# Other DRAM layouts for the block inverse, and separate tiles for values and receptance

## The chip, the cores and the metric

One core of one Trainium2 chip runs the kernel. TensorE multiplies matrices, VectorE, ScalarE and GpSimd work element by element, and SyncE (SP in the profile) issues most transfers between the core's SBUF and DRAM. The time is device microseconds of one execution. The kernel before took 1365.18 us, the median of three runs from 1364.78 to 1365.78.

## What is computed

Three layers follow one another, all in float32: a recurrence over 768 steps for 4 batches of 8 heads with a 40 x 40 state each, and two MLPs on its output, 3072 tokens of width 320 with 2048 hidden units.

```
for t in range(S):
    y[:, :, t] = einsum('bhd,bhde->bhe', rt, state)
    Sa = einsum('bhde,bhe->bhd', state, at)
    state = state * wt[:, :, None, :] - einsum('bhd,bhe->bhde', Sa, bt)
    state = state + einsum('bhd,bhe->bhde', vt, kt)
x = y.transpose(0, 2, 1, 3).reshape(B * S, H * D)
x = relu(x @ w_in) ** 2 @ w_out                      # first MLP
h = x @ w2_in
out = (h * clip(h + 3, 0, 6) / 6) @ w2_out           # second MLP
```

The weights come as 64-bit words and are converted to pairs of float32 in the kernel.

## The kernel before

The 768 steps are cut into 12 chunks of 64. A chunk of one batch is a *block* i = 4c + b (48 of them); it holds 8 heads as NP = 4 pairs p of two halves h, a half being 64 of the 128 partitions. Inside a block the recurrence is a unit lower triangular system of 64 steps for each head, and its inverse is needed before the block's states can be formed. The inverse is made for a whole chunk at once: 16 units u = (b, p), two halves h and two diagonal 32 x 32 blocks f of each 64 x 64 triangle, 64 triangles in all.

Where things lie:

- `TB` (ring of three, one per chunk) holds the triangles of a chunk, partition = 64 h + 32 f + row, free = unit and column. `f1a` (L595 to L606) makes two of its blocks with TensorE, ScalarE copies them, and after every second block L605 stores both to DRAM, tile `DT`, ordered row, half, unit, column.
- `inv_gen` (L626) reads the diagonal blocks back, one triangle per partition, into `ML` (L635, four transfers: the two lane groups q, each with f = 0 and 1). A lane group q computes every second column of each inverse. 31 steps of two instructions each (L645 multiply, L648 subtract) run on VectorE; chunk 1 has tiles of its own (`inv_e`) and runs on GpSimd. L650 transposes the result, L652 and L653 store it to `DIT` and `DI`, and L658 and L660 read it back to `TB` and to `AI` with rows on partitions.
- `merge_p` and `merge_x` (L663, L673) join the two 32 x 32 inverses of a head with TensorE; merge_p (L669) is the first reader of `AI` and of the returned `TB`.
- `VR` (ring of three) holds a block's values and receptance, `[104, 2, NP, 128]`, the two halves of a head pair in opposite columns; `load_main` (L547) loads it with one transfer per half (L552), and `VS` with another (L551). `umm` writes the block's solution into the free half of the value part, `gmm` (L708) multiplies value part by receptance part, `ys` (L728, L731) forms outputs and the state that follows (L735 to L737).

What runs when is written out by hand. A *slot* is one block: the string `ORDER` names its steps, and each `M` in it is one piece of the first MLP (`fill`), after which five steps of the waiting inverse are put on VectorE (`tick`). Blocks enter `f1` eight ahead of `ys`. After the fourth block of a chunk is prepared its inverse is begun: L635 is put on SyncE's queue, and the first L645 comes three slots' ends later in VectorE's program. Every engine takes its instructions in the order of the program, so a VectorE instruction that waits holds all that stand behind it, and a SyncE transfer that waits holds all later transfers of that queue. Besides this traffic SyncE's queue holds the loads of weight words (L83), the stores of converted weights (L137), the stores of the recurrence's output (L743) and the loads of the MLP's input (L188, L191). GpSimd loads the next block's inputs (L545) and ScalarE the converted weights (L162).

From about 285 to 870 us recurrence and first MLP run together; after that the second MLP runs alone.

Of the kernel before, what the change touches and what calls it, by code (L numbers as in the profile page):

```python
# [8 lines left out]
FP32 = mybir.dt.float32  # L9
# [460 lines left out]
def rwkv_moe_moe2_kernel(ctx, tc, pre_in, vr_in, v_in, nat, ident_d, mask_d, cst_d, w1_in, w1_out, w2_in, w2_out, out,  # L470
# [34 lines left out]
    AI = ring([128, NB, NP, 32], 2, "AI")  # L505
    VR = ring([104, 2, NP, 128], 3, "VR")
    RHS = ring([128, NP, 40], 1, "RHS")
    GV = ring([128, NP, 2, 104], 1, "GV")
    VS = ring([128, NP, 2, 40], NB, "VS")
    STK = ring([104, NP, 40], NB, "STK")  # L510
# [12 lines left out]
    U = NB * NP  # L523
    DT = [dram.tile([64, 2, U, 64], FP32, name=f"DT{k}") for k in range(2)]
    DI = [dram.tile([2 * U, 32, 2, 16], FP32, name=f"DI{k}") for k in range(2)]
    DIT = [dram.tile([4 * U, 32, 32], FP32, name=f"DIT{k}") for k in range(2)]

# [19 lines left out]
    def load_main(i):  # L547
        c, b = divmod(i, NB)
        for h, P in enumerate((PA, PB) if i < NS else ()):
            PV = slice(64, 128) if h == 0 else slice(0, 64)  # L550
            nc.sync.dma_start(out=VS[i % NB][PV, :, h, :], in_=v_in[c, b, h])  # L551
            nc.sync.dma_start(out=VR[i % 3][P, :, :, 64 - 64 * h:128 - 64 * h], in_=vr_in[c, b, h])  # L552

# [41 lines left out]
    def f1a(i):  # L595
        ps = f1_ps[i] = bank([128, NP, 128])
        rk, kb, tb = RK[i % RL], kb_of(i), tb_of(i)
        for p in range(NP):
            nc.tensor.matmul(ps[:, p, :], kb[:, p, :], rk[0:104, p, :], start=True, stop=True)  # L599
        for h in range(2):  # L600
            p = 64 * h
            nc.scalar.copy(out=tb[p:p + 64], in_=ps[p:p + 64, :, p:p + 64])
        c, b = divmod(i, NB)
        if b % 2:
            nc.sync.dma_start(out=DT[c % 2].rearrange("s h u t -> h s (u t)")[:, :, (b - 1) * NP * 64:(b + 1) * NP * 64],  # L605
                              in_=TB[c % 3][:, b - 1:b + 1].rearrange("p s a t -> p (s a t)"))  # L606

# [18 lines left out]
    def inv_gen(c, eng=nc.vector, ml=ML, inv=INV, tm=TMP):  # L626
# [6 lines left out]
        for q in range(2):  # L633
            for f in range(2):
                nc.sync.dma_start(out=ml[64 * q + 2 * U * f:64 * q + 2 * U * f + 2 * U],  # L635
                                  in_=dt_[32 * f:32 * f + 32, :, :, 32 * f:32 * f + 32].rearrange("s h u t -> (h u) s t"))
        iv = inv.rearrange("p a b -> p (a b)")
# [13 lines left out]
        for q in range(2):  # L651
            nc.sync.dma_start(out=dit.rearrange("l (k q) t -> q l k t", q=2)[q], in_=ml[64 * q:64 * q + 64, 0:16])  # L652
            nc.sync.dma_start(out=di[:, :, q, :], in_=inv[64 * q:64 * q + 2 * U])  # L653
        yield 1
        for h in range(2):
            (nc.gpsimd if c else nc.vector).memset(tb[64 * h + 32:64 * h + 64, :, 0:32], 0.0)
        for h, f, P, l in blocks:
            nc.sync.dma_start(out=tb[P, :, 32 * f:32 * f + 32], in_=dit[l:l + U].rearrange("u s t -> s u t"))  # L658
            if f == 0:
                nc.sync.dma_start(out=ai[P], in_=di[l:l + U].rearrange("u s q k -> s u (q k)"))  # L660
        yield
# [21 lines left out]
    def rhs(i):  # L683
        ps = bank([128, NP, 40])
        rk, vs = RK[i % RL], VS[i % NB]
        for p in range(NP):
            for h in range(2):
                nc.tensor.matmul(ps[64 * h:64 * h + 64, p, :], rk[:, p, 64 * h:64 * h + 64], vs[:, p, h, :],
                                 start=True, stop=True)
        nc.scalar.copy(out=RHS[0], in_=ps)  # L690

    def umm(i):
        ps = bank([104, NP, 64])
        tb, o = tb_of(i), VR[i % 3][:, 0]
        for p in range(NP):
# [9 lines left out]
    def gmm(i):  # L705
        ps = bank([128, NP, 128])
        for p in range(NP):
            nc.tensor.matmul(ps[:, p, :], VR[i % 3][:, 0, p, :], VR[i % 3][:, 1, p, :], start=True, stop=True)  # L708
        nc.vector.tensor_tensor(out=gv_of(i)[:, :, :, 0:64], in0=ps.rearrange("p a (h t) -> p a h t", h=2)[:, :, ::-1],
# [3 lines left out]
    def vumm(i):  # L713
        ps = bank([128, NP, 2, 64])
        pf = ps.rearrange("s p h e -> s p (h e)")
        for p in range(NP):
            nc.tensor.transpose(pf[:, p, 0:104], VR[i % 3][:, 0, p, :], ident[0:104, 0:104])
        nc.scalar.copy(out=gv_of(i)[:, :, :, 64:104], in_=ps[:, :, :, 0:40])

    def ys(i):  # L720
        ps = bank([104, NP, 104])
        c, b = divmod(i, NB)
        ktt, gv, sb, r0 = KT[i % (lag + 1)], gv_of(i), SB[b], VR[i % 3][:, 1]

# [4 lines left out]
        for p in range(NP):  # L729
            for h, P in enumerate((PA, PB)):  # L730
                nc.tensor.matmul(ps[P, p, 0:64], sb[P, p, :], r0[P, p, 64 - 64 * h:128 - 64 * h], start=False,  # L731
                                 stop=(p == NP - 1))
# [12 lines left out]
    def st(i):  # L745
# [9 lines left out]
        for h, P in enumerate((PA, PB)):  # L755
            nc.scalar.copy(out=nxt[P, :, h, :], in_=STK[b][P])

# [95 lines left out]
    with tc.manual_schedule():  # L853
# [45 lines left out]
        for k in range(0, NB, 2):  # L899
            pre_two(k)  # L900
            f1a(k)
            f1a(k + 1)
        for x in (VS[0], VR[0]):
            nc.vector.memset(x, 0.0)
# [7 lines left out]
        for k in range(NB):  # L912
            f1b(k)
            kt(k)
        for x in VS[1:] + VR[1:] + STK + SB:
            nc.gpsimd.memset(x, 0.0)
# [159 lines left out]
```

## Time and profile before

| what | value |
|---|---|
| median of the runs | 1365.18 us |
| the profiled execution | 1360.24 us, its span 1358.5 us |
| busy: TensorE, its weight loads, VectorE | 86%, 73%, 63% of the span |
| busy: ScalarE, GpSimd | 45%, 30% |
| mean granted TensorE clock | 0.915 of full speed |
| DMA packets | 253021, of which 201687 under 512 bytes |
| bytes moved | 146.97 MB, 108 GB/s over the span |

A busy share says how much of the span an engine had work; a wait says which other engine or transfer ended the idle time before an instruction. A transfer's row stands on the queue that issued it, and its length there is the issue alone; the landing shows in the row of the instruction that waits for it, or as a DMA piece of the chain of work. [...]

### The profile page before, as it was taken

To read this page: it belongs to the slowest core of one execution; us is meant where nothing else is said; L and a number is where in the kernel's file an instruction comes from. 1 tells how busy PE (TensorE), PEld (TensorE's weight loads), DVE (VectorE), ACT (ScalarE), POOL (GpSimd) and SP (SyncE) were. 2 spreads that over 40 slices of the span, in tenths; PEclk is the share of its full clock that TensorE was granted. 3 is DMA by queue.
4 is the path that set the end of the run, shared out by engine and by line. 5 is a ranking of instruction groups with operands and counts; after the bars stand their busy time and mean duration, and the time that the engine had idled before them with its cause. 6 is when DMAs were issued, how large, how long until landed. Compare 5 with 4: busy or idle time off the path is not lost.

```text
span 1358.5 us, 25814 instructions
## 1 busy us (share of the span) xinstructions
PE 1162.4 (86%) x9682; PEld 991.6 (73%) x9682; DVE 852.1 (63%) x1857; ACT 609.6 (45%) x1456; POOL 409.0 (30%) x601
## 2 busy tenths in 40 slices
PE   3177677898989798989888999978879999999994
PEld 3167567786768676877777788856668999999994
DVE  7838897858485848494949383359975434344432
ACT  4245555453445344544544343346654434344331
POOL 5685545343434343534343200024530000000000
PEclk9657867898999898999998899988989999999998
DMA  4546657554655555736463544265541010101000
GB/s 125 115 99 190 166 139 165 158 130 118 129 140 135 119 128 138 152 106 137 140 145 90 114 135 112 76 204 183 160 128 30 22 37 15 51 8 44 3 18 23
DMA packets 253021, 146.97 MB, mean 108 GB/s; under 512 B 201687, under 2 KB 216663, under 8 KB 252887
## 3 DMA queue, kind: packets, MB, share of 16 engines
q1 hardware_dynamic: 234327, 91.63, 28.7%
q10 hardware_dynamic: 13824, 37.75, 9.0%
q0 software_dynamic: 4736, 15.84, 4.1%
q8 instruction: 79, 1.29, 0.4%
q14 instruction: 55, 0.45, 0.1%
HBM read 115.30 MB, written 29.88 MB: 107 GB/s over the span
## 4 chain that ended last, share of the span: by engine, by line
PE 49%; DVE 17%; DMA 17%; SPq 4%; issue 4%; ACT 4%; POOL 3%; DVEq 0%; ACTq 0%; POOLq 0%
PE h L221 9%; DMA DT<-TB 6%; PE h L223 4%; PE o L262 4%; PE o L261 4%; PE o L260 4%; DVE TMP L645 3%; DVE INV L648 3%; PE o L248 2%; PE a L599 2%; PE h L224 2%; PE h L225 2%; DMA xr<-X 2%; PE o L249 2%; PE o L250 2%
## 5 line engine op out<-in xcount | busy, mean ns | idle before, releaser
L239 DVE TENSOR_TENSOR gs<-g,gs 128x512 fp32r<-128x512 f32 x192 | 149.7, 780 | 77.9 <-ACT gs L233 65.9
L645 DVE TENSOR_TENSOR TMP<-ML,INV 128x126 f32<-128x126 f32 (+22 forms) x341 | 111.6, 327 | 80.9 <-DMA ML<-DT 72.6
L614 POOL TENSOR_TENSOR RK<-RK,mask 64x256 f32<-64x256 f32 x96 | 74.9, 780 | 235.7 <-ACT RK L613 210.4
L231 DVE SCALAR_TENSOR_TENSOR g<-r,h 128x512 f32<-128x512 f32 x96 | 66.0, 687 | 120.2 <-ACT r L230 120.1
L105 POOL TENSOR_TENSOR bits<-res,bits 128x384 int32<-128x384 int32 (+1 forms) x64 | 67.8, 1064 | 204.9 <-DMA wl<-LI 122.3
L260 PE MATMUL o<-w_out,gs 128*128 128x320 f32 x384 | 119.5, 311 | 7.5 <-ACT os L837 5.4
L236 DVE TENSOR_TENSOR g<-r 128x512 f32<-128x512 f32 x96 | 65.7, 684 | 88.3 <-ACT r L235 88.2
L262 PE MATMUL o<-w_out,gs 128*128 128x320 f32 x384 | 120.0, 312 | 0.7 <-DVE gs L239 0.7
L230 ACT ACTIVATE r<-h,cst 128x512 f32<-128x512 f32 x96 | 66.1, 688 | 121.1 <-PE h L225 115.6
L261 PE MATMUL o<-w_lout,gs 128*128 128x320 f32 x384 | 119.3, 311 | 0.0
L648 DVE TENSOR_TENSOR INV<-INV,TMP 128x126 f32<-128x126 f32 (+22 forms) x341 | 111.7, 328 | 9.4 <-DMA VR<-in_vr_dram 0.4
L233 ACT CAST gs<-g 128x512 fp32r<-128x512 f32 x96 | 59.6, 620 | 82.9 <-DVE g L231 82.9
L575 POOL TENSOR_TENSOR RK<-IN,EE 40x256 f32<-40x256 f32 x82 | 67.3, 821 | 89.8 <-DVE EE L563 86.2
L221 PE MATMUL h<-xm,wl 128*128 128x512 f32 x192 | 78.5, 409 | 17.7 <-DMA wl<-LI 17.7
L235 ACT ACTIVATE r<-h 128x512 f32<-128x512 f32 x96 | 57.1, 594 | 81.4 <-PE h L225 71.9
L248 PE MATMUL o<-gs,wo_hi 128*128 128x512 f32 x192 | 88.7, 462 | 1.1 <-DVE os L837 1.1
L700 ACT ACTIVATE VR<-a 40x256 f32<-40x256 f32 x96 | 36.3, 378 | 109.4 <-PE a L698 108.9
L221 PE MATMUL h<-xm,wi_hi 128*128 128x512 f32 x192 | 84.8, 442 | 0.6 <-ACT xm L207 0.6
L260 PEld LDWEIGHTS o<-w_out,gs 128*128 128x128 f32 x384 | 72.6, 189 | 13.0 <-ACT os L837 5.8
L250 PE MATMUL o<-gs,wl 128*128 128x512 f32 x192 | 80.9, 421 | 1.2 <-DMA wl<-LO 1.2
L590 POOL TENSOR_TENSOR KBt<-IN,RV 104x256 f32<-104x256 f32 x78 | 72.9, 954 | 29.6 <-DVE INV L648 10.4
L249 PE MATMUL o<-gs,wo_hi 128*128 128x512 f32 x192 | 80.8, 421 | 0.1
(160 smaller groups left out, 2942.6 us busy)
## 6 DMA issues: line engine op xcount, KB each, us to landing
wl<-LI ACTq DMA_DIRECT2D x48, 384.0 KB
wl<-LO ACTq DMA_DIRECT2D x48, 384.0 KB
IN<-in_pre_dram POOLq DMA_DIRECT2D x37, 418.0 KB, 5.4
bits<-in_moe_w_in_dram SPq DMA_DIRECT2D x32, 384.0 KB
bits<-in_moe_w_out_dram SPq DMA_DIRECT2D x32, 320.0 KB
VR<-in_vr_dram SPq DMA_DIRECT2D x96, 80.0 KB
DT<-TB SPq DMA_DIRECT2D x24, 256.0 KB
xr<-X SPq DMA_DIRECT2D x12, 512.0 KB
```

Source lines behind the costliest of these rows:

```text
L221: nc.tensor.matmul(h, w[p][:, k], xm[:, k], start=(k + p == 0), stop=False)
L239: nc.vector.tensor_tensor(out=gs[:, 1], in0=g, in1=gs[:, 0].bitcast(FP32), op=ALU.subtract)
L248: nc.tensor.matmul(acc[d], hi, gs[:, 0], start=a, stop=False)
L249: nc.tensor.matmul(acc[d], hi, gs[:, 1], start=False, stop=False)
L250: nc.tensor.matmul(acc[d], lo, gs[:, 0], start=False, stop=z)
L260: nc.tensor.matmul(acc[q], gs[:, 0, s], hi, start=a, stop=False)
L261: nc.tensor.matmul(acc[q], gs[:, 0, s], lo, start=False, stop=False)
L262: nc.tensor.matmul(acc[q], gs[:, 1, s], hi, start=False, stop=z)
L590: e.tensor_tensor(out=kb_of(i)[:, :, 64 * x:64 * x + 64], in0=kb[:, :, x, :], in1=rr, op=ALU.mult)
L614: nc.gpsimd.tensor_tensor(out=o, in0=o, in1=mask[P].unsqueeze(1).to_broadcast([64, NP, 64]), op=ALU.mult)
L645: eng.tensor_tensor(out=tmp, in0=ml[:, s, s + 1:32].unsqueeze(2).to_broadcast([128, n, w]), in1=inv[:, s, 0:w].unsqueeze(1).to_broadcast([ ...
L648: eng.tensor_tensor(out=inv[:, s + 1:32, 0:w], in0=inv[:, s + 1:32, 0:w], in1=tmp, op=ALU.subtract)
```

## The change

- `DT` is laid out as diagonal block f, half, unit, row, column and holds the diagonal blocks alone. L605's one transfer per two blocks becomes four (half by diagonal block), and the read for a lane group q is one transfer of 64 triangles of 4 KB.
- `DIT` and `DI` have the lane group q as outermost dimension, so that the two stores of each are contiguous per triangle. The return reads then take one lane group each: eight transfers to `TB` (every second partition) where four stood, four to `AI` where two stood.
- `VR` is split into `VU` (values and solution) and `RZ` (receptance, halves outermost), and `VS` has its halves outermost. Values, receptance and `VS` are loaded with three transfers per half instead of two.

```diff
-    VR = ring([104, 2, NP, 128], 3, "VR")
+    VU = ring([104, NP, 128], 3, "VU")
+    RZ = ring([104, 2, NP, 64], 3, "RZ")
...
-    VS = ring([128, NP, 2, 40], NB, "VS")
+    VS = ring([128, 2, NP, 40], NB, "VS")
...
-    DT = [dram.tile([64, 2, U, 64], FP32, name=f"DT{k}") for k in range(2)]
-    DI = [dram.tile([2 * U, 32, 2, 16], FP32, name=f"DI{k}") for k in range(2)]
-    DIT = [dram.tile([4 * U, 32, 32], FP32, name=f"DIT{k}") for k in range(2)]
+    DT = [dram.tile([2, 2, U, 32, 32], FP32, name=f"DT{k}") for k in range(2)]
+    DI = [dram.tile([2, 2 * U, 32, 16], FP32, name=f"DI{k}") for k in range(2)]
+    DIT = [dram.tile([2, 4 * U, 16, 32], FP32, name=f"DIT{k}") for k in range(2)]
...
-            nc.sync.dma_start(out=VS[i % NB][PV, :, h, :], in_=v_in[c, b, h])
-            nc.sync.dma_start(out=VR[i % 3][P, :, :, 64 - 64 * h:128 - 64 * h], in_=vr_in[c, b, h])
+            nc.sync.dma_start(out=VS[i % NB][PV, h], in_=v_in[c, b, h])
+            nc.sync.dma_start(out=VU[i % 3][P, :, 64 - 64 * h:128 - 64 * h], in_=vr_in[c, b, h, :, 0])
+            nc.sync.dma_start(out=RZ[i % 3][P, 1 - h], in_=vr_in[c, b, h, :, 1])
...
-            nc.sync.dma_start(out=DT[c % 2].rearrange("s h u t -> h s (u t)")[:, :, (b - 1) * NP * 64:(b + 1) * NP * 64],
-                              in_=TB[c % 3][:, b - 1:b + 1].rearrange("p s a t -> p (s a t)"))
+            tb = TB[c % 3].rearrange("p s a t -> p (s a) t")
+            un = slice((b - 1) * NP, (b + 1) * NP)
+            for h in range(2):
+                for f in range(2):
+                    nc.sync.dma_start(out=DT[c % 2][f, h, un].rearrange("u s t -> s u t"),
+                                      in_=tb[64 * h + 32 * f:64 * h + 32 * f + 32, un, 32 * f:32 * f + 32])
...
-            for f in range(2):
-                nc.sync.dma_start(out=ml[64 * q + 2 * U * f:64 * q + 2 * U * f + 2 * U],
-                                  in_=dt_[32 * f:32 * f + 32, :, :, 32 * f:32 * f + 32].rearrange("s h u t -> (h u) s t"))
+            nc.sync.dma_start(out=ml[64 * q:64 * q + 4 * U], in_=dt_.rearrange("f h u s t -> (f h u) s t"))
...
-            nc.sync.dma_start(out=dit.rearrange("l (k q) t -> q l k t", q=2)[q], in_=ml[64 * q:64 * q + 64, 0:16])
-            nc.sync.dma_start(out=di[:, :, q, :], in_=inv[64 * q:64 * q + 2 * U])
+            nc.sync.dma_start(out=dit[q], in_=ml[64 * q:64 * q + 64, 0:16])
+            nc.sync.dma_start(out=di[q], in_=inv[64 * q:64 * q + 2 * U])
...
-            nc.sync.dma_start(out=tb[P, :, 32 * f:32 * f + 32], in_=dit[l:l + U].rearrange("u s t -> s u t"))
-            if f == 0:
-                nc.sync.dma_start(out=ai[P], in_=di[l:l + U].rearrange("u s q k -> s u (q k)"))
+            for q in range(2):
+                nc.sync.dma_start(out=tb[P.start + q:P.stop:2, :, 32 * f:32 * f + 32],
+                                  in_=dit[q, l:l + U].rearrange("u k t -> k u t"))
+                if f == 0:
+                    nc.sync.dma_start(out=ai[P, :, 16 * q:16 * q + 16], in_=di[q, l:l + U].rearrange("u s k -> s u k"))
...
-            nc.tensor.matmul(ps[:, p, :], VR[i % 3][:, 0, p, :], VR[i % 3][:, 1, p, :], start=True, stop=True)
+            nc.tensor.matmul(ps[:, p, :], VU[i % 3][:, p, :], RZ[i % 3][:, :, p, :], start=True, stop=True)
```

The other readers of `VR` and `VS` take the new names and dimensions; the memsets at the start that cleared a `VR` clear its `VU` and its `RZ`.

The engines that compute keep their order. SyncE's queue is what moves. First the place where chunk 6's blocks are stored and read back. A row is an issue: destination, source, shape, and xN for N alike. Numbers behind a name tell the copies of a tile apart. Before:

```order
L551 DMA VS_139<-in_v_dram 64x4x40
L552 DMA VR_136<-in_vr_dram 40x8x64
L551 DMA VS_139<-in_v_dram 64x4x40
L552 DMA VR_136<-in_vr_dram 40x8x64
L605 DMA DT_164<-TB_129 2x64x512
L635 DMA ML<-DT_164 32x32x32 x4
```

And now, on the same queue at the same place:

```order
L552 DMA VS_142<-in_v_dram 64x160
L553 DMA VU_136<-in_vr_dram 40x4x64
L554 DMA RZ_139<-in_vr_dram 40x256
L552 DMA VS_142<-in_v_dram 64x160
L553 DMA VU_136<-in_vr_dram 40x4x64
L554 DMA RZ_139<-in_vr_dram 40x256
L612 DMA DT_167<-TB_129 32x8x32 x4
L641 DMA ML<-DT_167 64x1024 x2
```

Six loads stand where four did, the store is four transfers instead of one, the read two instead of four; the order among them is the same.

The second place stands just ahead of the first: the return of the inverse of chunk 5, behind the output store of the slot. Before, on SyncE's queue:

```order
L743 DMA X_2_59<-XT_148 40x4x128 x2
L658 DMA TB_131<-DIT_169 32x16x32
L660 DMA AI_133<-DI_167 32x16x32
L658 DMA TB_131<-DIT_169 32x16x32
L660 DMA AI_133<-DI_167 32x16x32
L658 DMA TB_131<-DIT_169 32x16x32 x2
```

And now:

```order
L750 DMA X_2_59<-XT_151 40x4x128 x2
L664 DMA TB_131<-DIT_172 16x16x32
L667 DMA AI_133<-DI_170 32x16x16
L664 DMA TB_131<-DIT_172 16x16x32
L667 DMA AI_133<-DI_170 32x16x16
L664 DMA TB_131<-DIT_172 16x16x32
L667 DMA AI_133<-DI_170 32x16x16
L664 DMA TB_131<-DIT_172 16x16x32
L667 DMA AI_133<-DI_170 32x16x16
L664 DMA TB_131<-DIT_172 16x16x32 x4
```

Twelve issues stand where six did; the last piece of `AI` is the eighth of them, where it was the fourth.

## Rows read from the trace of the kernel before

**Rows 1.** Busy time by stretch: us, engines' busy us (instructions), clock, DMA share, GB/s.
```profile
285.00:870.00 585.00, 535.78 (x5520) 440.43 (x5520) 370.13 (x945) 269.30 (x717) 190.64 (x292) 0.95 0.52 126
...
292.00:322.00 30.00, 24.11 (x258) 19.63 (x258) 14.05 (x40) 10.29 (x28) 9.85 (x16) 0.89 0.57 134
...
763.00:803.00 40.00, 38.23 (x381) 31.12 (x381) 23.42 (x66) 18.94 (x48) 3.20 (x7) 0.96 0.47 121
sum 280.00, PE 245.60 PEld 201.66 DVE 162.14 ACT 125.64 POOL 95.42; mean PE 30.70 PEld 25.21 DVE 20.27 ACT 15.71 POOL 11.93
```

**Rows 2.** Waits, 285 to 870 us: engine, line <- releaser: total us, times, longest.
```profile
DVE TMP L645 <- DMA ML<-DT: 71.4, 8, 11.9
...
PE a L751 <- DVE STK L736: 27.2, 10, 5.9
```

**Rows 3.** Timeline, 411 to 446 us: start, length, engine, line, operation [idle before <-releaser].
```profile
418.19 0.31 SPq L658 DMA_DIRECT2D TB<-DIT  x1
...
420.35 4.87 SPq L658 DMA_DIRECT2D TB<-DIT  x2
...
426.35 0.65 PE L669 MATMUL a<-AI,TB 32*64 32x32 f32 x16
...
428.45 0.57 SPq L605 DMA_DIRECT2D DT<-TB  x1
...
439.79 1.06 PE L708 MATMUL a<-VR 104*128 104x128 f32 x8
439.84 2.27 SPq L635 DMA_DIRECT2D ML<-DT  x4
...
440.78 0.65 PE L669 MATMUL a<-AI,TB 32*64 32x32 f32 x16
...
445.58 0.19 DVE L645 TENSOR_TENSOR TMP<-ML,INV 128x31 f32<-128x31 f32 x1 [11.84 <-DMA ML<-DT]
```

**Rows 4.** Busy time by stretch of 3 us, right after that wait.
```profile
443.00:446.00 3.00, 0.00 (x0) 0.00 (x0) 0.33 (x2) 0.00 (x0) 0.00 (x0) 0.66 0.81 100
446.00:449.00 3.00, 1.73 (x7) 1.52 (x8) 2.83 (x13) 0.80 (x3) 0.22 (x1) 0.50 0.27 71
```

**Rows 5.** Transfers on the chain that ended last: start, us, what.
```profile
41.20 9.94 DMA DT<-TB
...
381.23 4.40 DMA xr<-X
...
495.73 9.41 DMA DT<-TB
...
814.67 4.38 DMA DI<-INV
...
963.32 2.34 DMA bits<-in_moe_w_out_dram
...
994.89 4.12 DMA X<-os
```

**Rows 6.** Issues on SyncE by line: ns min/median/max, first and last start.
```profile
L551 SPq DMA_DIRECT2D VS<-in_v_dram x96: 552/585/2672, 34.5 to 846.1; - x96
...
L552 SPq DMA_DIRECT2D VR<-in_vr_dram x96: 777/800/2431, 35.5 to 846.8; - x96
...
L658 SPq DMA_DIRECT2D TB<-DIT x48: 307/487/3173, 65.2 to 821.0; - x48
```

**Rows 7.** Timeline of the start, GpSimd's inverse and what stands behind it.
```profile
57.05 0.24 POOL L645 TENSOR_TENSOR inv_e<-inv_e 128x31 f32<-128x31 f32 x1 [9.65 <-DMA inv_e<-DT]
...
88.92 1.02 DVE L109 SCALAR_TENSOR_TENSOR res<-bits 128x384 f32<-128x384 f32 x1 [7.58 <-POOL bits L105]
...
92.33 1.62 PE L728 MATMUL a<-GV,KT 128*64 128x104 f32 x16 [7.00 <-DVE GV L709]
```

**Rows 8.** Waits of VectorE, 110 to 160 us.
```profile
DVE res L97 <- DMA bits<-in_moe_w_out_dram: 4.9, 1, 4.9
```

**Rows 9.** The page's DMA queues: packets, MB, share of 16 engines.
```profile
q1 hardware_dynamic: 234327, 91.63, 28.7%
```

More of the change, by code (lines that the diff above doesn't have):

```diff
@@ L687, in rhs @@
             for h in range(2):
-                nc.tensor.matmul(ps[64 * h:64 * h + 64, p, :], rk[:, p, 64 * h:64 * h + 64], vs[:, p, h, :],
+                nc.tensor.matmul(ps[64 * h:64 * h + 64, p, :], rk[:, p, 64 * h:64 * h + 64], vs[:, h, p, :],
                                  start=True, stop=True)
@@ L693, in umm @@
         ps = bank([104, NP, 64])
-        tb, o = tb_of(i), VR[i % 3][:, 0]
+        tb, o = tb_of(i), VU[i % 3]
         for p in range(NP):
@@ L716, in vumm @@
         for p in range(NP):
-            nc.tensor.transpose(pf[:, p, 0:104], VR[i % 3][:, 0, p, :], ident[0:104, 0:104])
+            nc.tensor.transpose(pf[:, p, 0:104], VU[i % 3][:, p, :], ident[0:104, 0:104])
         nc.scalar.copy(out=gv_of(i)[:, :, :, 64:104], in_=ps[:, :, :, 0:40])
@@ L722, in ys @@
         c, b = divmod(i, NB)
-        ktt, gv, sb, r0 = KT[i % (lag + 1)], gv_of(i), SB[b], VR[i % 3][:, 1]
+        ktt, gv, sb, r0 = KT[i % (lag + 1)], gv_of(i), SB[b], RZ[i % 3]
         PQ = (slice(0, 64), PB)
@@ L730, in ys @@
             for h, P in enumerate((PA, PB)):
-                nc.tensor.matmul(ps[P, p, 0:64], sb[P, p, :], r0[P, p, 64 - 64 * h:128 - 64 * h], start=False,
+                nc.tensor.matmul(ps[P, p, 0:64], sb[P, p, :], r0[P, 1 - h, p], start=False,
                                  stop=(p == NP - 1))
@@ L755, in st @@
         for h, P in enumerate((PA, PB)):
-            nc.scalar.copy(out=nxt[P, :, h, :], in_=STK[b][P])
+            nc.scalar.copy(out=nxt[P, h], in_=STK[b][P])
     gens = deque()
@@ L902, in rwkv_moe_moe2_kernel @@
             f1a(k + 1)
-        for x in (VS[0], VR[0]):
+        for x in (VS[0], VU[0], RZ[0]):
             nc.vector.memset(x, 0.0)
@@ L914, in rwkv_moe_moe2_kernel @@
             kt(k)
-        for x in VS[1:] + VR[1:] + STK + SB:
+        for x in VS[1:] + VU[1:] + RZ[1:] + STK + SB:
             nc.gpsimd.memset(x, 0.0)
```

## The prediction

> **What bounds the kernel now.** I read the page first (TensorE is the busiest engine by far), then the busy time by stage, then the waits of that stage, and last the timeline around one wait. The stage from 285 to 870 us, where recurrence and first MLP run together, has TensorE busy 535.78 of 585 us at a granted clock of 0.95 [rows 1]. So a gain has to come from its 49 us of idle time or from its clock. Its waits name two places: VectorE sits 71.4 us, in 8 pieces, before L645 until ML<-DT has landed, and TensorE sits 27.2 us before L751 for VectorE [rows 2]. They are one event, once for each chunk's inverse. SyncE stores the blocks (L605, DT<-TB), waits for the store, issues four reads of them (L635, ML<-DT), and VectorE, which takes its work in order, stands at the first step of the inverse.
>
> One event in full [rows 3]: the store is issued at 428.45, the first read only at 439.84, and VectorE starts at 445.58 after 11.84 us of waiting, so since 433.74. TensorE goes on with work that doesn't need VectorE until 441.43 (its last matmul group before the gap is the one at 440.78); 7.7 us of such a wait are covered, the rest is idle time of TensorE. [...]
>
> What all eight cost: the eight stretches of 30 or 40 us that begin with the store hold 280 us, TensorE busy 245.60 of them, so 34.4 idle [rows 1]. The other 305 us of the stage have 535.78 - 245.60 = 290.2 busy, 14.8 idle, 4.9%; at that rate the stretches would idle 13.6, so the excess is 20.8 us. The clock of the eight stretches, weighted by length, is 0.931 (rows from 0.89 to 0.98; the first and the last of the eight stand in [rows 1]); with 0.95 for the whole stage the other 305 us have 0.967. The difference over 280 us is 10 us of full-speed work. Together about **31 us** hang on this wait.
>
> **The change part by part.** VectorE, ScalarE, GpSimd and TensorE keep the order of their instructions; VR gives way to VU and RZ, and three memsets of it become six of half the size at the start, those of GpSimd ahead of its wait of 9.65 us for chunk 1's blocks [rows 7]. What changes is SyncE's queue, 633 rows before and 777 after with repeats joined, and the shape of its transfers.
>
> *The store of blocks.* One transfer of 256 KB becomes four of 32 KB that carry the diagonal blocks alone, in pieces of 128 bytes instead of 2 KB. Before, it takes 9.41 to 11.39 us from issue to the read that waits for it [rows 3, 5]. That is not what 256 KB cost in general: X<-os, 256 KB from 128 partitions, took 4.12 [rows 5]. The store's outermost dimension is the half, 2 long; after, it is 32 lanes. [...] New cost: three issues of 0.57 ahead of the last [rows 3], then the landing of small pieces, between 2.34 (a load of weight words, the fastest landing I quote) and 4.38 (DI<-INV, stores of 64-byte pieces) [rows 5]: 4.0 to 6.1 us. It saves 3.3 to 7.4; I take 5.2, the middle, since the store resembles DI<-INV in pieces but each of the four carries half the bytes.
>
> *The reads.* Four of 128 KB in 128-byte pieces become two of 256 KB in 4 KB pieces. Before: 445.58 - 439.84 = 5.74 us from first issue to VectorE's start [rows 3]. After: one issue of 0.3 to 0.6 and a landing between 2.34 (384 KB) and 4.40 (xr<-X, 768 KB in three) [rows 5], 2.7 to 5.0. It saves 0.7 to 3.0; I take 2.
>
> *What SyncE does ahead of the store.* The loads of values and receptance go from four to six per block. Before 2 x (0.585 + 0.800) = 2.77 us of issue [rows 6]. The values become one run per lane, the receptance too, and the third keeps strided halves with one dimension less. I take 0.4, 0.4 and 0.585 (a run of few dimensions costs between the 0.31 minimum of L658 and 0.585): 2.77, no change; bounds -0.4 to +1.9. The return of the inverse (TB<-DIT, AI<-DI) goes from six issues to twelve, of 0.487 each [rows 6]: 2.9 us more, in the slot just before the store. In the event above the burst began at 418.19 and the two last issues alone took 4.87, so the queue was held by the transfers and not by issuing [rows 3]; part of the 2.9 is then covered. I take 2 later; bounds 0 and 4.
>
> Sum for one event: 5.2 + 2 - 2 = **5.2 us earlier**, bounds -1 and 10. The mean wait of 71.4 / 8 = 8.9 us becomes 3.7, and the longest, 11.9, becomes 6.7. Both are inside the 7.7 us that TensorE covers, so nearly all of the 31 us come back: I take **28**; next late in these stretches is TensorE's own work. Bounds: 2 if an event moves by under 1 us, 43 if the 14.8 us idle in the rest of the stage, which follow from VectorE catching up after its wait, mostly go as well.
>
> *The start.* Chunk 1's inverse runs on GpSimd. Its store takes 9.94 us from 41.20 [rows 5], GpSimd waits 9.65 and starts at 57.05; behind its 62 steps stands the bits addition that VectorE's L109 waits 7.58 us for, and behind that the mask L709 for which TensorE waits 7.00 [rows 7]. Two stores become eight and the read moves as above, so the steps begin 5 to 8 us earlier and the 7.00 shrink by as much: **6**, bounds 0 and 7. The first inverse gains nothing: VectorE had other work until about when its blocks came.
>
> *Weight conversion, 110 to 285 us.* Loads of weight words are queued on SyncE behind the same store and reads; VectorE waited 4.9 us once for such words [rows 8], and for the stores of rests as well. I take **4**, bounds 0 and 10.
>
> *What it adds.* The merge of a block needs the first four reads of the inverse before and the first eight now, about 4 x 0.487 = 2 us later. In the event above the merge came at 426.35, 8.2 us after the burst began [rows 3]; eight issues (3.9) and a landing of up to 4.4 just fit. At the first and last inverse there is no such room: **-2**, bounds 0 and -40 (next part). The receptance operand of L708 is read in two runs of 64; no row shows that apart; the eight instructions of a block take 1.06 us [rows 3], and I take no change, at most a tenth of it, 5 us over 48 blocks. Packets of SyncE's queue, 234,327 for 28.7% of the engines' span [rows 9], fall by roughly 90,000 (4096 to 128 per inverse for ML alone), which is a gain that I don't count.
>
> Sum: 28 + 6 + 4 - 2 = **36 us**. The profiled execution took 1360.24 us, 1358.5 of it span; less 36 that is 1324. The median of the runs is 4.9 above it, 1365.18, and so **1329**.
>
> **Rivals.** *Small pieces eat the gain.* The change is meant to make pieces larger, but the block store goes from 2 KB to 128 bytes, and AI from 128 to 64. If its landing is at the slow end and SyncE's extra issues aren't covered, an event moves by 3.3 + 2 - 4, some 1 us only, long waits stay above 7.7, and about half of the 28 and of the 6 remain: 17 - 2 = 15, **1350**. For it: 64-byte stores took 4.38. Against: four reads in 4096 pieces of 128 bytes landed in 5.74 with their issues. [...]
>
> *The return leg becomes the wait (slower).* Twelve reads in 4096 pieces where six in 3072 stood, directly before the merge. It decides when the first eight need more than the 8.2 us of room. Twice the 7.0 us that the six took from 418.19 to 425.22 would put the eighth at 9.4 and its landing at 13.8, 5.6 late; on all eleven inverses that return inside the run 62 us, against which the 38 of gain stand: 1365 + 24 = **1389**; milder, 1375. Against: in this one event the queue was already crowded, and TensorE's waits hold no such wait in this stage.
>
> *Hidden anyway.* VectorE, not the wait, may set the pace: in the ticks of the inverse it runs almost without gaps. Then TensorE idles later what it doesn't idle now and only 2 us come out, **1363**. Against: VectorE is busy 370.13 of 585 us in this stage [rows 1].
>
> *More comes back.* The rest of the stage's idle time goes too: 43 + 7 + 6 = 56, **1309**.
>
> **How the numbers follow.** Forecast, 1315 to 1347: 0.64. Small pieces: 0.16. More comes back: 0.06. Hidden anyway: 0.06. Return leg: 0.08. The range takes the forecast, most of the first rival and of the larger gain: **1306 to 1354**, some 0.8. Faster by over 0.2%, which is about what a measurement of this kernel can tell from no change: 0.64 + 0.16 + 0.06 = 0.86; within it 0.06; slower 0.08.
>
> **What would show it.** In the trace after: store to first read below 7 us; the wait of VectorE for ML<-DT below 40 us in sum with none above 8; TensorE's wait for L736 near 10 or less; the clock of the stage 0.97 or more; GpSimd's first inverse step near 50; TensorE's merge L669 without new waits for AI. [...]

## The result, and the profile after

The changed kernel takes 1346.15 us (median of four runs, 1345.23 to 1348.39) beside 1364.98 for the kernel before: ratio 0.9864, 95% interval 0.9846 to 0.9881. That is 18.8 us faster, inside the range, and half of the 36 us that the sum gave. The profiled execution spans 1344.4 us.

The busy time by stretch of the kernel after answers to [rows 1], its waits from 285 to 870 us to [rows 2] (columns as there). The clock rose from 0.95 to 0.96 and no more. VectorE's wait for the blocks is not gone; it grew from 71.4 to 77.3 us.

```profile
285.00:870.00 585.00, 540.10 (x5554) 444.26 (x5553) 368.92 (x943) 268.17 (x709) 184.55 (x285) 0.96 0.46 122
```

```profile
DVE TMP L650 <- DMA ML<-DT: 77.3, 8, 10.3
PE a L758 <- DVE STK L743: 31.5, 12, 4.3
```

What the waits of SyncE's queue show is a change of cause. In the same stretch before, this one row led the waits on transfers:

```profile
SPq L635 <- DMA DT<-TB: 74.6, 8, 10.7
```

After, the wait for the store (L641) is small, and the list of waits on transfers is led by two others, before the fourth store (L612) and the `RZ` load (L554). Their releaser is `wl`, the converted weights that ScalarE loads for the MLP:

```profile
SPq L612 <- DMA wl<-LI: 35.7, 8, 5.0
SPq L554 <- DMA wl<-LO: 21.6, 9, 3.6
...
SPq L641 <- DMA DT<-TB: 9.7, 8, 1.3
...
SPq L664 <- DMA wl<-LI: 2.6, 1, 2.6
```

The event that answers to [rows 3] is the return of one inverse and the store and read of the next chunk's blocks. This is its timeline (start, length, engine, line, operation):

```profile
402.12 0.62 SPq L664 DMA_DIRECT2D TB<-DIT  x1
...
406.75 0.35 ACTq L162 DMA_DIRECT2D wl<-LI  x1
...
407.49 5.19 SPq L664 DMA_DIRECT2D TB<-DIT  x4
412.25 0.76 ACT L604 COPY TB<-a 64x256 f32<-64x256 f32 x2 [0.31 <-PE a L601]
...
415.21 0.51 SPq L553 DMA_DIRECT2D VU<-in_vr_dram  x1
416.42 0.33 ACTq L162 DMA_DIRECT2D wl<-LO  x1
419.39 0.29 SPq L554 DMA_DIRECT2D RZ<-in_vr_dram  x1
419.78 1.30 SPq L612 DMA_DIRECT2D DT<-TB  x3
421.18 0.33 ACTq L162 DMA_DIRECT2D wl<-LI  x1
426.12 0.30 SPq L612 DMA_DIRECT2D DT<-TB  x1
427.73 1.10 SPq L641 DMA_DIRECT2D ML<-DT  x2
...
432.54 0.19 DVE L650 TENSOR_TENSOR TMP<-ML,INV 128x31 f32<-128x31 f32 x1 [9.90 <-DMA ML<-DT]
```

The store itself is now fast: the last of its four transfers is issued at 426.12 and the read at 427.73, 1.61 us later, where 11.39 stood before. But ScalarE has the blocks ready at 413.01, and the last store goes out 13.1 us after that. SyncE stops three times on the way: inside the last four returns, between 415.72 and 419.39, and between 421.08 and 426.12. All three are put down to a load of `wl`: 2.6 us before L664, 3.6 before L554 and 5.0 before L612. Each of the last two ends 3 to 5 us after ScalarE issued such a load.

The chain's pieces that answer to [rows 5] show the faster store, and GpSimd's first inverse the earlier start of [rows 7], 4.65 us of waiting where 9.65 stood:

```profile
40.12 1.73 DMA DT<-TB
...
491.26 1.54 DMA DT<-TB
```

```profile
50.08 0.32 POOL L650 TENSOR_TENSOR inv_e<-inv_e 128x31 f32<-128x31 f32 x1 [4.65 <-DMA inv_e<-DT]
```

By stage: the first read of the fourth chunk's blocks starts at 303.85 before and at 293.41 after, 10.4 earlier. The first read of the last chunk's blocks starts at 772.67 and 758.41. Before:

```profile
303.85 2.27 SPq L635 DMA_DIRECT2D ML<-DT  x4
...
772.67 3.33 SPq L635 DMA_DIRECT2D ML<-DT  x4
```

After:

```profile
293.41 1.10 SPq L641 DMA_DIRECT2D ML<-DT  x2
...
758.41 1.10 SPq L641 DMA_DIRECT2D ML<-DT  x2
```

So from the first of the eight events to the last it takes 468.8 us before and 465.0 after. This length, called *eight events* below, is the measure of the steady stage; it comes from the one profiled execution of each kernel.

### The profile page after: what moved, and what is told of

The parts are those of the page before. It is cut to its first block, busy times and chain, and to the rows that moved or that the text cites. A ratio compares the mean times of both kernels' runs of the same rounds, so it can differ in the third digit from the quotient of the medians.

```text
span 1344.4 us, 26161 instructions
## 1 busy us (share of the span) xinstructions
PE 1160.4 (86%) x9682; PEld 989.1 (74%) x9682; DVE 855.7 (64%) x1858; ACT 609.4 (45%) x1456; POOL 407.3 (30%) x603
## 4 chain that ended last, share of the span: by engine, by line
PE 51%; DVE 24%; DMA 11%; issue 5%; SPq 4%; ACT 3%; POOL 1%; DVEq 0%; ACTq 0%; POOLq 0%
PE h L221 9%; PE h L223 5%; DVE INV L653 4%; DVE TMP L650 4%; PE o L262 4%; PE o L261 4%; PE o L260 4%; DVE res L109 2%; PE h L225 2%; PE h L224 2%; PE o L248 2%; DVE gs L239 2%; PE a L601 2%; PE o L249 2%; PE o L250 2%
## 5 line engine op out<-in xcount | busy, mean ns | idle before, releaser
L650 DVE TENSOR_TENSOR TMP<-ML,INV 128x126 f32<-128x126 f32 (+22 forms) x341 | 112.3, 329 | 85.6 <-DMA ML<-DT 77.3
L707 ACT ACTIVATE VU<-a 40x256 f32<-40x256 f32 x96 | 36.2, 378 | 115.0 <-PE a L705 114.5
```

The costliest lines, as they stand in the source:

```text
L650: eng.tensor_tensor(out=tmp, in0=ml[:, s, s + 1:32].unsqueeze(2).to_broadcast([128, n, w]), in1=inv[:, s, 0:w].unsqueeze(1).to_broadcast([ ...
```

## The experiments

Ratios are to the kernel before, timed beside each; line numbers shift a little from kernel to kernel, and code is cut at `...`. Theory A at first: the finer return leg, directly ahead of the store on SyncE's queue, took the gain back. Rival B: VectorE's pace sets the stage whatever the blocks do.

**The store and the read alone.** The kernel before with the new `DT`, its four stores and two reads:

```
+    DT = [dram.tile([2, 2, U, 32, 32], FP32, name=f"DT{k}") for k in range(2)]
...
+                    nc.sync.dma_start(out=DT[c % 2][f, h, un].rearrange("u s t -> s u t"), ...)
...
+            nc.sync.dma_start(out=ml[64 * q:64 * q + 4 * U], in_=dt_.rearrange("f h u s t -> (f h u) s t"))
```

> The store of the blocks and their read in the new layout alone; return of the inverse and loads as before. Theory A (the finer return leg, twelve transfers just ahead of the store, took back the gain of the steady stage): without it the four store issues take about 1.8 us also after a return, against 5.7 to 6.7 in the changed kernel, VectorE's wait for ML<-DT falls from 77 us to under 45 in sum, and the time is 1325 to 1338 us. Theory B (VectorE's pace or the weight loads set the stage anyway, the queue does not matter): the wait may shrink, the time stays at 1344 to 1349 as in the changed kernel.

1318.25 us, ratio 0.9646 (0.9614 to 0.9678): faster than the whole change, and below theory A's range too. The eight events take 440.7 us, and VectorE's wait is 46.5, just over the 45 expected. So rival B falls, and something in the rest of the change costs 28 us. One expectation failed: the four issues don't take 1.8 us but 2.8 to 5.3. SyncE stops before the fourth for a weight load here as well, only for less long:

```profile
SPq L609 <- DMA wl<-LO: 15.0, 7, 3.5
```

**The return alone.** The kernel before with the new `DIT` and `DI` and the twelve return reads:

```
+            nc.sync.dma_start(out=dit[q], in_=ml[64 * q:64 * q + 64, 0:16])
+            nc.sync.dma_start(out=di[q], in_=inv[64 * q:64 * q + 2 * U])
...
+            for q in range(2):
+                nc.sync.dma_start(out=tb[P.start + q:P.stop:2, :, 32 * f:32 * f + 32], ...)
+                if f == 0:
+                    nc.sync.dma_start(out=ai[P, :, 16 * q:16 * q + 16], ...)
```

> The layout of DIT and DI and the twelve return transfers alone; store, read and loads as before. Theory A: the burst of the return grows from about 4 to 7 us to 9 to 11, the store behind it is issued 3 to 5 us later, VectorE's wait for ML<-DT grows by about 3 us per chunk, and the time is 1370 to 1385 us. Theory B: no change, 1363 to 1367.

1376.50 us, ratio 1.0079 (1.0049 to 1.0109), slower; eight events 475.7. The burst takes 8.9 us in the mean of the eight where it took 4.3; the store ends its issue 1.3 us later behind ScalarE's copy and VectorE waits 1.4 us longer, both less than expected.

**The loads alone.** `VU`, `RZ` and `VS` as in the change, all else as before:

```
+            nc.sync.dma_start(out=VS[i % NB][PV, h], in_=v_in[c, b, h])
+            nc.sync.dma_start(out=VU[i % 3][P, :, 64 - 64 * h:128 - 64 * h], in_=vr_in[c, b, h, :, 0])
+            nc.sync.dma_start(out=RZ[i % 3][P, 1 - h], in_=vr_in[c, b, h, :, 1])
```

> The split of VR into VU and RZ and the contiguous VS alone. Both theories: six issues of 0.31 to 0.52 us instead of four of 0.58 and 0.80, about the same issue time per block, fewer and larger pieces; 1361 to 1367 us. A third possibility, that six transfers instead of four hold up the queue by themselves (each transfer waits for the one eight before it), gives 1368 to 1375.

1367.16 us, ratio 0.9989 (0.9970 to 1.0008): nothing.

**All but the return.** The change with the return leg of before.

```
-            for q in range(2):
-                nc.sync.dma_start(out=tb[P.start + q:P.stop:2, :, 32 * f:32 * f + 32],
-                                  in_=dit[q, l:l + U].rearrange("u k t -> k u t"))
-                if f == 0:
-                    nc.sync.dma_start(out=ai[P, :, 16 * q:16 * q + 16], ...)
+            nc.sync.dma_start(out=tb[P, :, 32 * f:32 * f + 32], in_=dit[l:l + U].rearrange("u s t -> s u t"))
+            if f == 0:
+                nc.sync.dma_start(out=ai[P], in_=di[l:l + U].rearrange("u s q k -> s u (q k)"))
```

> The changed kernel with the return of the inverse put back as before (six transfers, DIT and DI in the old layout). Theory A: the store's four issues take about 2 us, the wait for ML<-DT is under 40 us in sum, 1322 to 1336 us. Theory B: 1344 to 1349. If the six loads per block and not the return hold the store, the four store issues still take 4 us or more and the time is 1338 to 1346.

1310.31 us, ratio 0.9577 (0.9545 to 0.9610), 36 us below the changed kernel and again below theory A's range; eight events 439.2. Its waits, 285 to 870 us, and the same event:

```profile
DVE TMP L649 <- DMA ML<-DT: 42.1, 8, 6.7
```

```profile
399.11 3.36 SPq L662 DMA_DIRECT2D TB<-DIT  x2
...
406.84 1.80 SPq L611 DMA_DIRECT2D DT<-TB  x4
410.83 1.10 SPq L640 DMA_DIRECT2D ML<-DT  x2
```

The four stores go out in 1.80 us instead of 6.64. Theory A holds as to the place. It doesn't say what in the return costs so much.

**Why the old store was slow.** The store of before, split into one transfer for each half, nothing else:

```
-            nc.sync.dma_start(out=DT[c % 2].rearrange("s h u t -> h s (u t)")[:, :, (b - 1) * NP * 64:(b + 1) * NP * 64],
-                              in_=TB[c % 3][:, b - 1:b + 1].rearrange("p s a t -> p (s a t)"))
+            for h in range(2):
+                nc.sync.dma_start(out=DT[c % 2][:, h].rearrange("s u t -> s (u t)")[:, (b - 1) * NP * 64:(b + 1) * NP * 64],
+                                  in_=TB[c % 3][64 * h:64 * h + 64, b - 1:b + 1].rearrange("p s a t -> p (s a t)"))
```

> Only the store of the kernel before is altered: one transfer for both halves of a block pair becomes one for each half. Rows in DRAM stay pieces of 2 KB, the same bytes move, and the read stays as before (four transfers of 128-byte pieces). Spread theory: the old store was slow (9.4 to 11.4 us from issue to landing) because its outermost dimension is 2, and the new one is fast (1.5 to 1.7) because its outermost dimension is 32. Then each half, with 64 rows outermost, lands in 2 to 4 us, the waits of VectorE on the read fall from 72.6 us to 40 to 55, and the time is 1322 to 1340 us, most of what the store and read alone gave (1318). Rival, bytes and layout: the store became fast because it moves half the bytes and is read in whole triangles; then the landing stays at 8 us or more and the time is 1355 to 1366.

1323.67 us, ratio 0.9675 (0.9651 to 0.9699); eight events 444.4. The same bytes in the same 2-KB pieces now land in 2.45 to 4.17 us, as pieces of its chain show:

```profile
38.86 2.45 DMA DT<-TB
278.81 3.41 DMA DT<-TB
534.15 4.17 DMA DT<-TB
```

So it was the one transfer with an outermost dimension of 2 that was slow, not its bytes or the places in DRAM. The traces also have its completion counter rise otherwise than those of the new stores: the store issued at 428.45 in the kernel before has marks at 429.44, 439.75 and 439.82, and each of the 24 stores there has three, one about 1 us after the issue and two at the landing; each of the 96 stores of the changed kernel has sixteen. What a mark stands for was not shown. The split alone brings more than twice the gain of the change.

**Which part of the return.** First the change with `DI` and the two reads of `AI` as before, then the change with `DIT` and the four reads of `TB` as before:

```
-                if f == 0:
-                    nc.sync.dma_start(out=ai[P, :, 16 * q:16 * q + 16], ...)
+            if f == 0:
+                nc.sync.dma_start(out=ai[P], in_=di[l:l + U].rearrange("u s q k -> s u (q k)"))
```

```
-            for q in range(2):
-                nc.sync.dma_start(out=tb[P.start + q:P.stop:2, :, 32 * f:32 * f + 32], ...)
+            nc.sync.dma_start(out=tb[P, :, 32 * f:32 * f + 32], in_=dit[l:l + U].rearrange("u s t -> s u t"))
```

> The changed kernel with the part of the return that goes to AI as before: DI in its old layout, two reads of AI with pieces of 128 bytes; the eight reads of TB by lanes stay. Ten transfers return where twelve did in the changed kernel (1346 us) and six in the one with the whole return as before (1310). Theory that the cost goes by the number of transfers in the burst: burst 9 to 10 us, time 1330 to 1340. Rival, the 64-byte pieces of AI: then nearly all comes back, 1310 to 1318. Rival, the reads to every second partition of TB: then nothing comes back, 1342 to 1350.

> The changed kernel with the part of the return that goes to TB as before: DIT in its old layout, four reads of TB; the four reads of AI by lanes, with pieces of 64 bytes, stay. Eight transfers return. Theory that the cost goes by the number of transfers in the burst: burst 8 to 8.5 us, stores behind it issue in 2 to 5 us, time 1316 to 1328. Rival, the 64-byte pieces of AI: 1338 to 1348. Rival, the reads to every second partition of TB: 1308 to 1314.

With eight reads of `TB` by lanes: 1346.07 us, ratio 0.9844 (0.9815 to 0.9873), eight events 465.3, as slow as the whole change. With four reads of `AI`: 1318.15, 0.9644 (0.9613 to 0.9675), 442.9. The first fits the rival of the reads to every second partition, the second the theory of the number, and the cost doesn't grow evenly with the number of transfers (six, eight, ten, twelve give 1310, 1318, 1346, 1346). Here I suspected the reads to every second partition, and went back to SyncE's waits and to the built program.

**What SyncE waits for.** The trace names the completion counter of each transfer. In the kernel before and in the changed kernel the transfers of SyncE and ScalarE (728 and 944 issues) take eight counters in turn, 101, 103 to 108 and 110, and before a counter is taken again its engine has waited for it, and so for the transfer eight places before. In the event above the second `RZ` load takes 107 at 419.39; the `wl` load issued at 416.42 had it before, and its last mark is at 419.33. The fourth store takes 103 at 426.12, after the `wl` load issued at 421.18, whose last mark is at 426.10. The places, with the loads of `wl` among them, are set when the program is built. Of the transfers from the burst to the read these follow a weight load by eight places, in most or all of the eight events:

```
before:                          AI read after LO, VR load after LI, third ML read after LO
changed kernel, lanes in TB:     TB or AI reads after LO and LI, last RZ load after LO, fourth DT store after LI
all but the return:              AI read after LO (in three events a VU load after LI)
store and read alone:            AI read after LO, fourth DT store after LO (in three a VR load after LI)
four reads of AI:                reads after LO and LI, VS or VU load after LI, third or fourth DT store after LO
```

This is what the waits above say (L612 for `wl<-LI`, L554 for `wl<-LO`): SyncE stands until a load has landed that ScalarE, at its own pace in the MLP, has only just issued, here 3.0 and 4.9 us before. A tie as such costs little: the two kernels at 1318 us have one at a store too, with shorter stops (eight events 440.7 and 442.9), and all but the return (439.2) has its long stops behind the read, where the event no longer needs the queue:

```profile
SPq L552 <- DMA wl<-LI: 40.7, 8, 6.1
```

Theory C: this sharing, shifted by the added transfers, is what took the gain. It makes two predictions that the number of transfers doesn't: ten transfers with other places are harmless, and twelve are harmless if the weight loads don't share.

```
-            nc.sync.dma_start(out=tb[P, :, 32 * f:32 * f + 32], in_=dit[l:l + U].rearrange("u s t -> s u t"))
+            for g in range(2):
+                nc.sync.dma_start(out=tb[P, U // 2 * g:U // 2 * g + U // 2, 32 * f:32 * f + 32],
+                                  in_=dit[l + U // 2 * g:l + U // 2 * g + U // 2].rearrange("u s t -> s u t"))
```

> The kernel with the return as before (1310 us), with each of the four reads of TB cut into two by units instead of by lanes: 32 consecutive partitions each, DIT in its old layout. Ten transfers return, in pieces of 128 bytes and with the same bytes as in the kernel with the finer TB part (1346 us), whose eight reads went to every second partition. Theory of the shared counters: SyncE's and ScalarE's transfers take eight completion semaphores in turn, and in the 1346 kernel the fourth store to DT takes the one that a load of converted weights (wl<-LI, ScalarE's queue) has, so SyncE waits for that load; in this program the load's place in the turn falls two later and no store waits for it: 1308 to 1320, four stores issued in about 1.8 us. Theory of the number of transfers: 1335 to 1348. Theory of the lanes (reads to every second partition are slow): 1308 to 1320 as well, so this run tells the number from the other two.

1320.13 us, ratio 0.9666 (0.9627 to 0.9706), eight events 439.8, at the upper end of what theory C expected. With ten return reads, by units, no store and no `RZ` load follows a weight load by eight places, and the four stores go out in 1.91:

```profile
402.81 4.56 SPq L663 DMA_DIRECT2D TB<-DIT  x4
...
410.52 1.91 SPq L611 DMA_DIRECT2D DT<-TB  x4
```

So the number as such costs nothing in the eight events (439.2 with six); the whole time is 10 us above the 1310.31. That the lanes land slowly is still open by this run.

**The weight loads on GpSimd's queue.** In the traces of the kernel before and of the changed kernel GpSimd's transfers take eight other counters, 111 to 118, so a weight load on its queue should hold up no transfer of SyncE.

> The changed kernel (1346 us) with the loads of converted weights (wl, L162) issued by GpSimd's queue instead of ScalarE's. GpSimd's queue has completion semaphores of its own, so no transfer of SyncE waits for a weight load any more; the twelve return reads stay as they are. Theory of the shared counters: the burst of returns takes some 7 us instead of 10.6, the four stores to DT 1.8 to 2.5 instead of 6.6, the waits of VectorE on the read 35 to 50 us instead of 77, time 1305 to 1325. Theories of the number or of the lanes: the burst and the stores stay as long as they were, 1338 to 1350. Against both: GpSimd gets to the loads later than ScalarE did, and TensorE waits for weights; then the time is above 1346 and weight loads stand in TensorE's waits.

```
-        self.nc.scalar.dma_start(out=t.bitcast(FP32), in_=w["lo" if part else "li"][f // 2])
+        self.nc.gpsimd.dma_start(out=t.bitcast(FP32), in_=w["lo" if part else "li"][f // 2])
```

1331.74 us, ratio 0.9763 (0.9724 to 0.9802), eight events 443.6 instead of 465.0, with all twelve reads in place; from 285 to 870 us none of SyncE's waits is put down to a weight load. Busy time, waits and the event:

```profile
285.00:870.00 585.00, 546.74 (x5660) 448.53 (x5659) 390.54 (x968) 281.58 (x742) 235.95 (x375) 0.99 0.49 130
```

```profile
DVE TMP L649 <- DMA ML<-DT: 44.8, 8, 6.8
PE a L757 <- DVE STK L742: 12.0, 15, 3.0
```

```profile
408.35 3.81 SPq L663 DMA_DIRECT2D TB<-DIT  x4
...
416.77 1.79 SPq L611 DMA_DIRECT2D DT<-TB  x4
```

The stores take 1.79 us, the wait falls from 77.3 to 44.8 and the clock reaches 0.99. This speaks for theory C, and it can't be the lanes, which are as they were. But the time lies between the ranges of theory C and of its rivals, and the burst takes 8.9 us in the event, more than the 7 expected. The total stays 21 us above the kernel without the new return: 11.8 of them are lost before the fourth chunk's read (295.4 beside 283.6).

Two more kernels price the move itself.

> The kernel before (1366 us) with the same move of the weight loads to GpSimd's queue. It prices the move by itself. Theory of the shared counters: in the program before the reads of ML share with loads of wl, older ones, so there is little to free: 1352 to 1368. If the move costs by itself (GpSimd late with weights), above 1370.

> The kernel with the return as before and all else changed (1310 us), with the weight loads on GpSimd's queue. Theory of the shared counters: without sharing the finer return costs only its issues, so this kernel and the changed one with the same move lie within 10 us of each other, both at 1300 to 1325; the 36 us between 1346 and 1310 are gone. Theories of the number or of the lanes: this one 1300 to 1315, the changed one with the move 25 us or more above it.

The kernel before with the move: 1369.57, ratio 1.0028 (1.0010 to 1.0047), eight events 463.3; the time lies just above the 1352 to 1368 expected. All but the return with the move: 1312.99, ratio 0.9619 (0.9582 to 0.9655), 428.8. Here my expectation that the two moved kernels lie within 10 us failed: 18.8 us remain between 1331.74 and 1312.99. In the eight events the return costs 465.0 - 439.2 = 25.8 us with the weight loads on ScalarE's queue and 443.6 - 428.8 = 14.8 with them on GpSimd's. So about 11 of the 26 go with the sharing, as far as the move does nothing else; 15 stay with the twelve reads. The burst holds SyncE from 403.25 to 412.16 with the new return, and from 396.52 to 400.87 with the old. VectorE's waits in the second of the two moved kernels are these:

```profile
DVE TMP L649 <- DMA ML<-DT: 26.1, 7, 6.5
DVE TMP L649 <- POOL RK L574: 7.1, 1, 7.1
```

The last row is the eighth event's wait for the read as well: the read is marked landed at 665.83, and VectorE starts at 665.96. So the new return makes this wait (44.8 - 33.2) / 8 = 1.5 us longer in the mean. Whether the 15 are the number of issues or the lanes these runs don't tell, nor why ten reads by units cost nothing like it in the eight events.

**The store on another queue.** All but the return, with the four stores issued by ScalarE behind its own copy:

```
-                    nc.sync.dma_start(out=DT[c % 2][f, h, un].rearrange("u s t -> s u t"), ...)
+                    nc.scalar.dma_start(out=DT[c % 2][f, h, un].rearrange("u s t -> s u t"), ...)
```

> The kernel with the return as before and all else changed (1310 us), with its four stores to DT issued by ScalarE right behind the copy that feeds them instead of by SyncE. There the copy ended at 403.6 us, the first store was issued at 406.84 behind a return burst and six loads, and the read at 410.83. Theory that SyncE's queue ahead of the store is what is left of the waits (42 us on the read): store issue right at the copy's end, read 3 to 4 us sooner, waits on the read 15 to 28 us, time 1285 to 1302. Rival: the issues take 1.8 us or more of ScalarE's time in each of 24 places, and VectorE and TensorE wait for ScalarE instead: 1305 to 1325.

1288.01 us, ratio 0.9415 (0.9391 to 0.9438), the fastest kernel here. Eight events take 414.5 us and the wait is nearly gone:

```profile
285.00:870.00 585.00, 562.54 (x5728) 463.08 (x5725) 421.79 (x1010) 296.76 (x773) 208.93 (x304) 0.99 0.54 141
```

```profile
DVE TMP L649 <- DMA ML<-DT: 5.1, 5, 2.2
```

ScalarE pays for the issues: it does no other work for 20.0 us in this stage, before the copy that follows the stores, where the profile shows nothing that it waits for. That is less than is won:

```profile
ACT RK L619 <- issue: 20.0, 11, 2.6
```

The move also shifts the places in the turn, which was not separated from it.

## Why the prediction came out as it did

Sign and range were right, the place was not, and that the time fell into the range is partly luck. The profiled spans differ by 14.1 us: 10.4 of them are won before the fourth chunk's read and 3.8 in the eight events, where the sum had 10 and 28. The step that failed is the one on SyncE's queue ahead of the store.

- **The store.** Taken 5.2 us from the first issue to the read, bounds 3.3 to 7.4. Where SyncE isn't stopped between the four issues, in all but the return, this takes 4.04 us in the mean of the eight events instead of 9.97, so 5.9 less: the size was right. In the changed kernel it is 7.44, since the fourth store is held up. From the last issue alone the event has 1.61 instead of 11.39, 9.8 less. The prediction set the store's outermost dimension, 2 before and 32 after, beside its time. The split store bears this out: the same bytes in the same pieces, with 64 rows outermost in each half, land in 2.45 to 4.17 us, and the kernel's ratio is 0.9675. Whether two transfers in place of one have a part in that was not shown; one over 128 partitions was not run.
- **The reads.** Taken 2, bounds 0.7 to 3.0; in the event 5.74 before, 432.54 - 427.73 = 4.81 after, so 0.9, and 1.7 in the mean of the eight. The reads alone don't set it: in all but the return the same two take 418.85 - 410.83 = 8.02, and there a weight load is issued 0.25 us behind them. Whether that is the cause was not tested.
- **What SyncE does ahead of the store: the step that failed.** Taken 2 us later, bounds 0 and 4. From the copy's end to the last store's issue it is 428.45 - 424.10 = 4.35 us before and 426.12 - 413.01 = 13.11 after, 8.8 later. I counted issues and their length. The queue held by "the transfers and not by issuing" stood in my own text, but I took it as cover for the new issues; I didn't ask which transfer each issue waits for. All three stops are put down to ScalarE's weight loads. One event: 9.8 + 0.9 - 8.8 = 1.9 us instead of 5.2, and its wait is 9.90 instead of 11.84. This event was one of the worst before. In the mean of all eight, and by the prediction's own terms, the first store goes out 7.1 us behind the copy instead of 2.1, so 5.0 later; the store's term gives 2.5 and the reads 1.7, and VectorE's wait is 0.7 longer: 77.3 / 8 = 9.7 us beside 8.9. (The bounds of the event's sum were also drawn too narrow: by its terms they are -1.9 and 10.8.)
- **What hangs on the wait.** 31 us, 28 of them to be had, was right in size: with the wait at a longest of 6.7 us (all but the return) the eight events are 29.7 shorter, TensorE's wait for STK is gone from the head of the list, and the clock is 0.99. The 7.7 us of [rows 3] divide the kernels: the longest wait is 10 us or more in all that take 463 us and more for the eight events, and at most 7.5 in all at 445 and less. In the changed kernel it is 10.3, and from 435 to 438 us TensorE works at a mean granted clock of 0.53, much as at the 0.50 of [rows 4]. But a wait below 7.7 isn't free, as the prediction took it: with the store on ScalarE's queue the waits, none of them above 6.7 before it, fall from 42.1 us to 5.1, and the eight events are another 24.7 us shorter, as far as that move does nothing else.

```profile
435.00:438.00 3.00, 3.00 (x8) 2.27 (x8) 3.00 (x10) 1.20 (x4) 1.35 (x2) 0.53 0.63 188
```

- **Start and weight conversion.** Taken 6 and 4; the fourth chunk's read comes 10.4 us earlier. Right in sum, but without the new return it is 20.3 (283.57), so these stages had 10 more to give, which the return took. By what way was not settled; ScalarE's first weight load is at 253.3 us, and with the loads on GpSimd's queue the read comes no earlier (295.4), so the sharing can hardly be it.
- **Adds.** The merge waits 0.6 us for AI, 0.4 before (and 4.4, in four pieces, once the weight loads are moved); the two-run operand costs nothing, 1.06 us for the eight matmuls as in [rows 3]; the loads cost nothing.
- **Small pieces eat the gain.** The time (1350) is close to what came, and for another reason: stores in 128-byte pieces landed in 1.54 to 1.73 us on the changed kernel's chain. `AI` in pieces of 64 bytes with its two more reads costs 8 us (1318 beside 1310), but there a store also follows a weight load, so the pieces can't be priced apart.
- **The return leg becomes the wait.** Half right. The new return alone is slower than before, 1376.5, near the mild case of 1375. But the place was wrong: the merge waits 0.4 us there; it is the store behind the burst that goes out late. Both sides stood on one queue, and I weighed the return only for its reader.
- **Hidden anyway** falls with the store and read alone. **More comes back** (1309) is what all but the return gave in number, not in its parts: 29.7 us in the eight events and 20.3 before them, where 43 and 13 were set.

## What to carry to other kernels

When transfers are added to a queue, ask not only how long they take to issue but what each of them, and each that follows, must wait for before it may start: here a counter shared with ScalarE's queue held SyncE for up to 5.0 us at the fourth store, while none of the eight events of the kernel before has its store tied to a weight load. Test the parts of a layout change one by one: here one part was worth 48 us, another took 36 back (1346 beside 1310), and a line that only splits a transfer along its outermost dimension brought most. A store that feeds a round trip is worth trying on the queue of the engine that makes its data, if the other queue carries bursts; here it brought 22 us more.

## What the runs showed of the hardware

At one size of pieces the shape of the transfer made the difference here: 256 KB in 2-KB pieces took 7.9 to 11.4 us in the kernel before as one transfer with an outermost dimension of 2, its landing marked in two steps (the chain has pieces of 7.92 and 8.95 besides the 9.41 that the prediction took as the least), and 2.45 to 4.17 us as two transfers whose outermost dimension is 64, as pieces of the split store's chain. In the changed kernel stores of 32 KB in 128-byte pieces from 32 lanes landed in sixteen steps each, the last 1.50 to 5.40 us after the issue, 1.71 in the median.

SyncE's queue stood while the transfer engines were mostly idle: in the changed kernel it is stopped from 415.72 to 419.39 us, and from 415 to 418 the DMA share (next to last column; the time of the packets over that of 16 engines) is 0.32, while it is 1.06 from 415 to 418 in the kernel before, just ahead of its burst. After and before:

```profile
415.00:418.00 3.00, 3.00 (x31) 2.53 (x31) 2.84 (x4) 2.18 (x7) 2.86 (x4) 1.00 0.32 91
```

```profile
415.00:418.00 3.00, 3.00 (x39) 2.35 (x39) 2.40 (x5) 1.23 (x3) 2.51 (x3) 1.00 1.06 187
```
